# The MLP's second product of the chunk pairs by seven block products

## Chip, cores and metric

One core of one Trainium2 chip. The metric is the device time of one execution in microseconds; before the change the median of three runs is 830.9 us. Engines are named as in the profile: PE (TensorE), DVE (VectorE), ACT (ScalarE), POOL (GpSimd), SP (SyncE, which issues nearly all DMAs here).

## The reference

Attention with a window of 64 positions, then a mixer: two products over the tokens, then two over the channels. All data are float32.

```python
x = attention(q, k, v)                    # (8, 576, 512)
h = np.maximum(xt @ w_tok1, 0.0) @ w_tok2
u = x + h.transpose(0, 2, 1)
h2 = np.maximum(u @ w_ch1, 0.0) @ w_ch2   # 512 -> 1536 -> 512
return (u + h2)
```

## The kernel before the change

The attention and the token products take the first 257 us or so. What follows is the channel MLP: `u` is cut into nine chunks of 512 tokens, kept in DRAM as `u_dram[j]` with the 512 channels as four blocks of 128 partitions.

**Precision.** A float32 operand is split into a high part in the type that PE takes (`hi`, a copy on ACT that rounds) and a low part (`lo` = operand - `hi`, a subtraction on DVE). A block product is three matmuls: weight hi x data hi, weight hi x data lo, weight lo x data hi. Weights are 128x128, data 128x512, and a product of 128x512 fills one PSUM bank of eight.

**Plain chunks** (0, 1, 2): `gemm1` makes hidden block `ft` (of 12) from four channel blocks, 12 matmuls; `relu_split` makes the hi and lo parts of its ReLU on ACT and DVE. `gemm2` sums over hidden blocks into the four output blocks, and `add_out` adds them to `u` and stores. While chunk 1 runs, a generator (`weight_steps`) makes the sums of `w1` that the next part needs, a step after each hidden block, and stores them as `w1s` in DRAM.

**Chunk pairs** (3,4), (5,6), (7,8): here the first product is already done by Strassen's scheme in Winograd's form. The 2x2 blocks are channel halves, hidden halves and the two chunks; seven products `m1` to `m7` take the place of eight. `pair_f(q, f)` makes the four hidden blocks (`f` and `f + 6`, of each chunk) with 7 x 6 = 42 matmuls in four banks P, Q, R, S, in the order m1, m6, m7, m5, m2, m4, m3. Products share banks: `m2` is accumulated on top of `m1` in P, `m4` on `m7` in R, `m3` on `m5` in S. So the bank must have been read before the later product starts: x1 (a copy of P by ACT), x1 + Q, x2 = x1 + R, x3 = x2 + S, and later x2, x1 again, all on DVE. The data operands of the seven products (`comb`, tags c0 to c6) are hi and lo parts of sums of `u` blocks: `load_raw` loads raw blocks, `sums` and `sum4` form the sums on DVE, `prep` splits them. For the next pair this is done in the last f of a pair and in the second product behind it.

After every two f (a **group**, three in a pair) comes the second product as before Strassen: eight outputs (two chunks, four channel blocks) in eight banks, each a sum over the four hidden blocks made, 8 x 4 x 3 = 96 matmuls, and eight `add_out`. The whole of `w2` stays in SBUF as hi and lo parts (`w2hi`, `w2lo`).

**Order.** The program's order on each engine is that in which the code is written; nothing is moved. Each engine works strictly in its order, and a DMA waits in SP's order. `w1s` comes in slots of one f (three of them, `load_w1`, two DMAs of 896 KB), loaded again when its f is done.

## Time and profile before

| | |
|---|---|
| runs | 829.18, 830.9, 831.1 us |
| profiled execution | 829.17 us, its span 827.4 us, granted PE clock 0.999 |
| attention and token products | to about 257 us |
| chunk 0 | about 257 to 324 us |
| chunks 1, 2 | 324.2 to 389.5 and 389.5 to 454.7 us |
| pairs | 454.7, 577.8 and 700.8 us, the last to the end |
| HBM traffic | 164 GB/s over the span |

The profile gives the busy time of each engine, groups of equal instructions with mean duration and the idle time before them, a timeline, windows (busy time of each engine in a stretch), and the chain of waits that ended last. Matmuls overlap, so the duration of one (0.39 us) is longer than the distance from one to the next.

### The profile page before, as it was taken

To read this page: it belongs to the slowest core of one execution; us is meant where nothing else is said; L and a number is where in the kernel's file an instruction comes from. 1 tells how busy PE (TensorE), PEld (TensorE's weight loads), DVE (VectorE), ACT (ScalarE), POOL (GpSimd) and SP (SyncE) were. 2 spreads that over 40 slices of the span, in tenths; PEclk is the share of its full clock that TensorE was granted. 3 is DMA by queue.
4 is the path that set the end of the run, shared out by engine and by line. 5 is a ranking of instruction groups with operands and counts; after the bars stand their busy time and mean duration, and the time that the engine had idled before them with its cause. 6 is when DMAs were issued, how large, how long until landed. Compare 5 with 4: busy or idle time off the path is not lost.

```text
span 827.4 us, 15250 instructions
## 1 busy us (share of the span) xinstructions
PE 814.4 (98%) x5860; PEld 676.9 (82%) x5860; DVE 511.1 (62%) x1365; ACT 336.6 (41%) x1014; POOL 106.5 (13%) x117
## 2 busy tenths in 40 slices
PE   8989999999999999999999999999999999999998
PEld 6758888888889878888888888878888878888886
DVE  5987899799773993773444535277625277525352
ACT  6988989888864530331221202032202033202020
POOL 3632534444330000000000000000000000000000
PEclk9999999999999999999999999999999999999999
DMA  9847778777645629634506443334433234432002
GB/s 354 284 148 243 237 243 291 231 228 276 193 132 174 193 65 273 185 96 136 182 1 237 143 180 111 118 111 171 170 159 135 95 131 167 176 137 90 1 1 101
DMA packets 69672, 136.51 MB, mean 165 GB/s; under 512 B 7008, under 2 KB 39264, under 8 KB 67680
## 3 DMA queue, kind: packets, MB, share of 16 engines
q1 hardware_dynamic: 67488, 133.71, 47.4%
q10 hardware_dynamic: 2112, 1.84, 0.7%
q8 instruction: 46, 0.75, 0.4%
q14 instruction: 26, 0.21, 0.1%
HBM read 104.66 MB, written 30.87 MB: 164 GB/s over the span
## 4 chain that ended last, share of the span: by engine, by line
PE 84%; DVE 8%; ACT 4%; issue 2%; DMA 1%; POOL 0%; POOLq 0%; DVEq 0%; SPq 0%; ACTq 0%
PE gp L847 19%; PE op L635 11%; PE gp L627 8%; PE h L364 5%; PE up L412 5%; PE op_4a L635 4%; PE op_2b L635 4%; PE op_2a L635 4%; PE op_0b L635 4%; PE op_0a L635 4%; PE op_4b L635 4%; PE xp L316 4%; PE s L274 3%; PE pp L304 3%; PE up L405 2%; ACT e L297 2%
## 5 line engine op out<-in xcount | busy, mean ns | idle before, releaser
L847 PE MATMUL gp<-m,w1hi 128*128 128x512 f32 x504 | 155.3, 390 | 0.7 <-DVE x L855 0.7
L297 ACT ACTIVATE e<-e,nm 128x128 f32<-128x128 f32 x288 | 112.2, 397 | 6.5 <-DVE nm L289 6.3
L847 PEld LDWEIGHTS gp<-m,w1hi 128*128 128x128 f32 x504 | 94.5, 188 | 21.0 <-DVE x L855 1.5
L847 PE MATMUL gp<-m,w1lo 128*128 128x512 f32 x252 | 98.0, 389 | 0.0
L614 ACT ACTIVATE ghi<-x 128x512 fp32r<-128x512 f32 x54 | 34.1, 632 | 119.9 <-DVE x L857 68.3
L289 DVE CUSTOM_DVE_ANT_0 e<-s,mask 128x128 f32<-128x128 f32 x288 | 65.3, 285 | 10.6 <-PE s L274 10.5
L851 ACT COPY x<-gp 128x512 f32<-128x512 f32 x18 | 10.4, 578 | 143.3 <-PE gp L847 143.3
L615 DVE SCALAR_TENSOR_TENSOR glo<-x,ghi 128x512 fp32r<-128x512 f32 x54 | 37.4, 692 | 38.1 <-ACT ghi L614 38.1
L614 ACT ACTIVATE ghi<-gp 128x512 fp32r<-128x512 f32 x50 | 29.9, 597 | 70.0 <-PE gp L627 70.0
L627 PE MATMUL gp<-uhi,w1lo 128*128 128x512 f32 x144 | 56.0, 389 | 0.0
L627 PE MATMUL gp<-ulo,w1hi 128*128 128x512 f32 x144 | 56.0, 389 | 0.0
L627 PE MATMUL gp<-uhi,w1hi 128*128 128x512 f32 x144 | 56.0, 389 | 0.0
L297 ACT ACTIVATION_READ_ACCUMULATOR e<-e,nm 128x1 f32 x288 | 55.9, 194 | 0.0
L847 PEld LDWEIGHTS gp<-m,w1lo 128*128 128x128 f32 x252 | 47.3, 188 | 9.9
L615 DVE SCALAR_TENSOR_TENSOR glo<-gp,ghi 128x512 fp32r<-128x512 f32 x50 | 34.4, 688 | 25.4 <-ACT ghi L614 25.3
L635 PE MATMUL op<-glo,w2hi 128*128 128x512 f32 x128 | 49.8, 389 | 0.0
L635 PE MATMUL op<-ghi,w2hi 128*128 128x512 f32 x128 | 49.8, 389 | 0.0
L635 PE MATMUL op<-ghi,w2lo 128*128 128x512 f32 x128 | 49.8, 389 | 0.0
L316 PEld LDWEIGHTS xp<-v,pt 128*64 128x64 f32 x1152 | 36.6, 138 | 12.9 <-ACT e L297 9.4
L104 POOL TENSOR_TENSOR xlo<-x,xhi 128x512 fp32r<-128x512 f32 x32 | 41.6, 1300 | 43.6 <-ACT xhi L101 42.9
L304 PE MATMUL pp<-ident,e 128*128 128x128 f32 x288 | 45.4, 282 | 1.5
L274 PE MATMUL s<-k,q 64*64 64x128 f32 x1152 | 41.8, 277 | 2.6 <-DMA k<-kh 0.9
(161 smaller groups left out, 1827.9 us busy)
## 6 DMA issues: line engine op xcount, KB each, us to landing
v<-vh SPq DMA_DIRECT2D x36, 512.0 KB, 4.4
w1hi<-w1s SPq DMA_DIRECT2D x18, 896.0 KB, 4.7
w1lo<-w1s SPq DMA_DIRECT2D x18, 896.0 KB, 6.5
raw<-wc SPq DMA_DIRECT2D x32, 384.0 KB, 4.6
q<-qh SPq DMA_DIRECT2D x36, 256.0 KB, 4.7
k<-kh SPq DMA_DIRECT2D x7, 1280.0 KB, 7.7
out<-uf SPq DMA_DIRECT2D x35, 256.0 KB, 2.7
uf<-u_dram SPq DMA_DIRECT2D x8, 1024.0 KB, 9.1
```

What stands on the lines that cost most here:

```text
L104: eng_lo.tensor_sub(lo, src, hi.bitcast(F32))
L274: nc.tensor.matmul(so, qt[r, j, half], kbs[b][r, n:n + 2, j], start=True, stop=True)
L289: nc.vector.tensor_tensor_reduce(out=e[:, h], in0=s[:, h], in1=mk, scale=-scale, scalar=MAX_F32, op0=ALU.add, op1=ALU.min, accum_out=nm[:, ...
L297: nc.scalar.activation(e[:, h], e[:, h], AF.Exp, bias=nm[:, g:g + 1], scale=-1.0, accum_out=sm[:, g:g + 1])
L304: nc.tensor.transpose(pp[:, h], e[:, h], ident)
L316: nc.tensor.matmul(xp[half * BLK:(half + 1) * BLK, h], pts[h % 2][:, h // 2, half * BLK:(half + 1) * BLK], vt[:, half, h], start=True, sto ...
L364: nc.tensor.matmul(h_ps[b][tt], w[:, o + tt * P:o + (tt + 1) * P], x, start=first and n == 0, stop=last and n == len(combos) - 1)
L614: nc.scalar.activation(hi, src, AF.Relu)
L615: nc.vector.scalar_tensor_tensor(out=lo, in0=src, scalar=0.0, in1=hi.bitcast(F32), op0=ALU.max, op1=ALU.subtract)
L627: nc.tensor.matmul(gp, w[:, w1_at(ft, ct)], x[:, ct], start=(k == 0), stop=(k == 3 * NCT - 1))
L635: nc.tensor.matmul(op, w[:, ct, ft], x[:, cols], start=(first and k == 0), stop=(last and k == 3 * len(gs) - 1), skip_group_check=not (fir ...
L847: nc.tensor.matmul(b, w[:, at], c[:, h, t], start=(n < 4 and k == 0), stop=(k == 5), skip_group_check=True)
```

## The change

The second product of the pairs is done by the same seven products: blocks are output channel halves (t counts the two blocks in a half), hidden halves and chunks. A group takes 2 (t) x 7 x 2 (f) x 3 = 84 matmuls (`pair_op`), t = 0 in banks of the even set, t = 1 of the odd one, with the same sharing of banks. The seven data operands are sums of the four hidden blocks of an f:

- `block` takes the ReLU of a hidden block into SBUF as float32 (`made`: r11, r12, r22, r21; the names that the rows show as `w2hi_r` and `w2lo_r`, in room that the end of `w2` leaves). For m1, m2, m3 it also makes the hi part (ACT) and the lo part (DVE for m1, POOL for m2 and m3).
- `combine(fi)` makes the other four (sums t1, t2, r12 - in place - and t1 again on DVE, their hi parts on ACT, their lo parts on DVE). For the even f it runs step by step between the products of the odd f, for the odd f at once in the second product, behind the products that need only the even f.
- Parts that two t's and groups share are added into `ufs` as banks are read; m1 + m6 is kept in `common` and added to three outputs only in the last group (by POOL, at the program's end by DVE). There are 14 reads of banks in a group, and 6 more additions in the last.

The sums of `w2` are made in chunk 1 (`weight_steps2`, 31 steps, from `w2_dram`, which now gets all of `w2`), its plain quarters are stored in chunk 2 (`quarter_steps2`), and `load_w2s` brings a slot for each t and group, two DMAs of 896 KB. `w1` has two slots instead of three. `Columns` is a tensor in several tiles, so that a part can be used again by itself. Half of the lo parts of `prep` for the next pair go to POOL.

```diff
-SLOT, NSLOT = NPROD * 2 * P, 3
+SLOT, NSLOT = NPROD * 2 * P, 2
+NGRP = NH // 2
...
+        def weight_steps2():
...
+                nc.vector.tensor_add(s1, s1, a)
+                hi("m5")
+                yield
+                nc.vector.tensor_sub(a, c, a)
+                hi("m7")
+                lo("m5")
+                yield
...
+        def load_w2s(n):
+            if n < (NCHUNK - N_PLAIN) // 2 * NGRP * 2:
+                grp, t = n // 2 % NGRP, n % 2
+                for k, w in enumerate((w2hf, w2lf)):
+                    nc.sync.dma_start(w[:, t * SLOT:(t + 1) * SLOT].bitcast(F32),
+                                      w2s[k][:, grp, t].rearrange("p m f c -> p (m f c)"))
...
                     if j == 1:
                         next(steps, None)
+                        if half == 1 and ft % 2:
+                            next(steps2, None)
+                    if last and half == 0:
+                        next(steps3, None)
...
-                    load_w1(2)
...
                     if j == 1:
                         next(steps, None)
+                        for _ in range((2, 5)[half]):
+                            next(steps2, None)
...
+        def combine(fi):
+            r, sub = made, nc.vector.tensor_sub
+            sub(r["t1"], r["r12"], r["r11"])
+            parts_hi(fi, "m5")
+            yield
+            sub(r["t2"], r["r22"], r["t1"])
+            parts_hi(fi, "m6")
+            yield
+            sub(r["r12"], r["r22"], r["r12"])
+            parts_hi(fi, "m7")
+            yield
+            parts_lo(fi, "m6", nc.vector)
+            yield
+            parts_lo(fi, "m5", nc.vector)
+            yield
+            sub(r["t1"], r["r21"], r["t2"])
+            parts_hi(fi, "m4")
+            yield
+            parts_lo(fi, "m7", nc.vector)
+            yield
+            parts_lo(fi, "m4", nc.vector)
...
+            def block(name, src, m, eng):
+                nc.scalar.activation(made[name], src, AF.Relu)
+                if m:
+                    parts_hi(fi, m)
+                    parts_lo(fi, m, eng)
...
                     nc.vector.tensor_add(x3, b, x2)
-                    done(1, f + NH, x3)
+                    block("r22", x3, "m3", nc.gpsimd)
                 elif m == "m2":
-                    done(0, f, b)
+                    block("r11", b, "m1", nc.vector)
                 elif m == "m4":
                     nc.vector.tensor_add(x2, b, x1)
-                    done(0, f + NH, x2)
+                    block("r21", x2, "m2", nc.gpsimd)
                 else:
                     nc.vector.tensor_add(x1, b, x1)
-                    done(1, f, x1)
+                    block("r12", x1, None, None)
+                next(rest, None)
+                if q + 1 < len(pairs):
+                    if f == NH - 2 and m == "m1":
+                        sums()
+                    if f == NH - 1 and n < 4:
+                        prep(q + 1, m, 0, nc.gpsimd if n % 2 else nc.vector)
+        def pair_op(q, grp, ufs, more, final):
...
+            for t in range(2):
+                for fi in range(2):
+                    product(t, "m1", fi)
+            for m in PRODUCTS[1:4]:
+                for t in range(2):
+                    product(t, m, 0)
+            for _ in combine(1):
+                pass
+            if more:
+                for m in PRODUCTS[4:]:
+                    if m == "m4":
+                        sum4()
+                    prep(q + 1, m, 0, nc.gpsimd if m == "m4" else nc.vector)
+                load_raw(q + 1, 1)
+            for t in range(2):
...
+                    if m != "m1" and (m != "m2" or not end):
+                        for fi in (1,) if m in PRODUCTS[:4] else (0, 1):
+                            product(t, m, fi)
+                    if m == "m1" and grp == 0:
+                        nc.scalar.copy(common[t], b)
+                    elif m in ("m1", "m6"):
+                        nc.vector.tensor_add(common[t], b, common[t])
+                    elif m == "m7":
+                        add(1, 2 + t, b)
...
+                    if more and t == 1 and m == "m1":
+                        sums()
+                    if more and t == 1:
+                        if m == "m4":
+                            sum4()
+                        prep(q + 1, m, 1, nc.gpsimd if m in ("m7", "m2", "m3") else nc.vector)
+                load_w2s((q * NGRP + grp + 1) * 2 + t)
```

How the order moves, at three places. First DVE in the odd f of the first pair's second group (f = 3), before:

```order
L853 TENSOR_TENSOR x_0_3_6418<-gp_3_1_6415,x_0_3_6418 128x512
L855 TENSOR_TENSOR x_0_3_6419<-gp_3_2_6416,x_0_3_6418 128x512
L857 TENSOR_TENSOR x_0_3_6420<-gp_3_3_6417,x_0_3_6419 128x512
L615 SCALAR_TENSOR_TENSOR glo_9_6450<-x_0_3_6420,ghi_9_6449 128x512
L615 SCALAR_TENSOR_TENSOR glo_3_6460<-gp_3_0_6414,ghi_3_6459 128x512
L862 TENSOR_TENSOR x_0_3_6419<-gp_3_2_6416,x_0_3_6418 128x512
L615 SCALAR_TENSOR_TENSOR glo_9_6471<-x_0_3_6419,ghi_9_6470 128x512
L865 TENSOR_TENSOR x_0_3_6418<-gp_3_3_6417,x_0_3_6418 128x512
```

Now the same stretch begins with the even f's `combine` (L964 to L977 are its sums, L959 a lo part, `gp` a bank of the f):

```order
L964 TENSOR_TENSOR w2lo_r<-w2hi_r 128x512
L967 TENSOR_TENSOR w2lo_r<-w2hi_r,w2lo_r 128x512
L1011 TENSOR_TENSOR x_1_6268<-gp_3_1_6612,x_1_6268 128x512
L970 TENSOR_TENSOR w2hi_r<-w2hi_r 128x512
L1013 TENSOR_TENSOR x_0_6269<-gp_3_2_6613,x_1_6268 128x512
L959 TENSOR_TENSOR gloc_6254<-w2lo_r,ghic_6253 128x512
L1015 TENSOR_TENSOR x_0_6270<-gp_3_3_6614,x_0_6269 128x512
L959 TENSOR_TENSOR gloc_6258<-w2lo_r,ghic_6257 128x512
L959 TENSOR_TENSOR w1lo_69<-w2hi_r,w1hi_67 128x512
L977 TENSOR_TENSOR w2lo_r<-w2hi_r,w2lo_r 128x512
L1020 TENSOR_TENSOR x_0_6269<-gp_3_2_6613,x_1_6268 128x512
L959 TENSOR_TENSOR gloc_6256<-w2hi_r,ghic_6255 128x512
```

Between the five reads of banks stand nine other instructions now (two more rows, L1023 and L959, end the f), where there were four lo parts.

Second ACT in the last f of the first pair (f = 5), before (`m` is a hi part for the next pair, `ghi` one of a hidden block):

```order
L851 COPY x_0_5_6686<-gp_5_0_6682 128x512
L101 CAST m_1_6699<-r_1_0_6599 128x512
L101 CAST m_1_6709<-t_1_0_6608 128x512
L101 CAST m_1_6719<-r_1_0_6601 128x512
L614 ACTIVATE ghi_11_6729<-x_0_5_6688 128x512
L101 CAST m_1_6733<-t_1_0_6607 128x512
L614 ACTIVATE ghi_5_6742<-gp_5_0_6682 128x512
```

and now (L955 is a hi part for the second product, L126 one for the next pair, L991 a ReLU into `made`):

```order
L991 ACTIVATE w2hi_r<-x_0_6267 128x512
L955 CAST ghic_6257<-w2lo_r 128x512
L1009 COPY x_1_6268<-gp_5_0_6876 128x512
L955 CAST ghic_6253<-w2lo_r 128x512
L126 CAST m_1_6891<-r_1_0_6537 128x512
L955 CAST ghic_6255<-w2hi_r 128x512
L126 CAST m_1_6903<-t_1_0_6546 128x512
L126 CAST m_1_6914<-r_1_0_6539 128x512
L991 ACTIVATE w2hi_r<-x_0_6270 128x512
L955 CAST w2hi_4552<-w2hi_r 128x512
L126 CAST m_1_6928<-t_1_0_6545 128x512
L991 ACTIVATE w2hi_r<-gp_5_0_6876 128x512
```

The copy of bank P and the ReLUs stand behind hi parts that wait for DVE's sums.

Third DVE in the second product of that last group, before: the eight reads of banks stood alone behind the preps. Now, from the end of `combine(1)` on (L129 a lo part for the next pair, L857 `sum4`, L1077 and L1045 reads of banks of t = 0):

```order
L959 TENSOR_TENSOR gloc_6266<-w2lo_r,ghic_6265 128x512
L129 TENSOR_TENSOR m_1_7014<-r_1_0_6543,m_1_7014 128x512
L857 TENSOR_TENSOR r_1_0_6537<-r_1_0_6543,t_1_0_6546 128x512
L129 TENSOR_TENSOR m_1_7021<-r_1_0_6541,m_1_7021 128x512
L1077 TENSOR_TENSOR w2lo_r<-op_2_0_0_6964,w2lo_r 128x512
L1077 TENSOR_TENSOR w2lo_r<-op_2_0_1_6965,w2lo_r 128x512
L1045 TENSOR_TENSOR uf_6335<-op_2_0_2_6966,uf_6335 128x512
L1045 TENSOR_TENSOR uf_6335<-op_2_0_3_6967,uf_6335 128x512
```

PE's products m2, m4 and m3 of t = 0 go into the banks that the fifth, seventh and eighth row read, and wait for them.

More of the change, by code (lines that the diff above doesn't have):

```diff
@@ L633, in gemm2 @@
             for ft, (ghi, glo) in zip(fts, gs):
-                for w, x in ((w2hi, ghi), (w2hi, glo), (w2lo, ghi)):
-                    nc.tensor.matmul(op, w[:, ct, ft], x[:, cols], start=(first and k == 0),
+                at = slice((ct * NFT + ft) * P, (ct * NFT + ft + 1) * P)
+                for w, x in ((w2hf, ghi), (w2hf, glo), (w2lf, ghi)):
+                    nc.tensor.matmul(op, w[:, at], x[:, cols], start=(first and k == 0),
                                      stop=(last and k == 3 * len(gs) - 1), skip_group_check=not (first and last))
@@ new lines, in mixer_kernel @@
+        whole = [t[:, n] for t in whole for n in range(4)]
+        behind = [[w[:, NSLOT * SLOT + n * CHUNK:NSLOT * SLOT + (n + 1) * CHUNK] for n in range(5)] for w in (w1hi, w1lo)]
+        behind += [w[:, NSLOT * SLOT:NSLOT * SLOT + CHUNK] for w in (w2hf, w2lf)]
+        spare = [new_g(f"c{n}") for n in range(8)]
+        ops_g = [dict(zip(PRODUCTS, spare[:7])),
+                 dict(zip(PRODUCTS, [*zip(behind[0], behind[1]), spare[7], tuple(behind[2:])]))]
+        made = dict(zip(("r11", "r12", "r22", "r21", "t1", "t2"), whole))
```

194 lines of the change are left out of this document (139 added, 55 removed).

## Prediction

> **What bounds the kernel now.** I read the page first, then the chain that ended last, then the engines' rows in the pairs.
>
> ```profile
> PE 814.4 (98%) x5860; PEld 676.9 (82%) x5860; DVE 511.1 (62%) x1365; ACT 336.6 (41%) x1014; POOL 106.5 (13%) x117
> ...
> 700.80 19.04 PE gp L847 x84
> 719.84 5.44 PE op_0a L635 x24
> ...
> 736.16 5.44 PE op_0b L635 x24
> 741.60 19.04 PE gp L847 x84
> ```
>
> The first row is the page's, the others are the chain of waits of the third pair's first group. TensorE is the bound and never waits there: two f take 19.04 us for 84 matmuls, the second product 4 x 5.44 = 21.76 us for 96. That is **0.2267 us a matmul**. The mean of 390 ns that the page gives counts overlapping matmuls, and a saving worked out with it would be too large by 1.7.
>
> ```profile
> 454.70:577.80 123.10, 122.76 (x542) 101.35 (x541) 64.44 (x99) 25.82 (x44) 0.00 (x0) 1.00 0.38 137
> 577.80:700.80 123.00, 122.66 (x541) 101.27 (x540) 65.62 (x101) 25.82 (x44) 0.00 (x0) 1.00 0.40 142
> 700.80:822.00 121.20, 121.20 (x538) 100.39 (x537) 53.26 (x80) 18.17 (x30) 0.00 (x0) 1.00 0.23 86
> ```
>
> These are windows of the three pairs (length, then PE, PEld, DVE, ACT, POOL busy). DVE has half its time free and POOL all of it; only in the first two pairs does PE lose 0.34 us.
>
> **What goes.** The second product of a group falls from 96 matmuls to 84, over nine groups 108 matmuls: 108 x 0.2267 = **24.5 us less**. The profiled execution took 829.2 us (span 827.4 and 1.8 around it; the median shown is 830.9), so without new waits 804.7.
>
> **What comes in the pairs.** The order rows show it. A group's DVE had 18 + 8 = 26 instructions; now 2 x 14 + 14 = 42, of which 18 have two SBUF inputs. Their pace:
>
> ```profile
> 548.53 0.68 DVE L745 TENSOR_TENSOR t<-r,r 128x512 f32<-128x512 f32 x1
> 549.25 0.69 DVE L747 TENSOR_TENSOR r<-r,r 128x512 f32<-128x512 f32 x1
> 549.85 0.69 DVE L748 TENSOR_TENSOR t<-r,t 128x512 f32<-128x512 f32 x1
> ...
> 551.66 0.68 DVE L104 TENSOR_TENSOR m<-t,m 128x512 fp32r<-128x512 f32 x1
> 552.26 0.69 DVE L855 TENSOR_TENSOR x<-gp,x 128x512 f32<-128x512 f32 x1
> ```
> ```profile
> 553.00 0.74 PE L847 MATMUL gp<-m,w1hi 128*128 128x512 f32 x2 [0.34 <-DVE x L855]
> ```
>
> DVE starts one every 0.60 us, 0.72 where it needs the one before; PE starts 0.05 us after the DVE instruction that it waits for (552.26 + 0.69 to 553.00). So 42 x 0.60 = 25 us fit in the group's new 38.1 us (168 x 0.2267). **As a sum the work fits; as a chain it does not.** The chain runs over ScalarE:
>
> ```profile
> 553.46 0.69 DVE L857 TENSOR_TENSOR x<-gp,x 128x512 f32<-128x512 f32 x1
> 554.84 0.69 DVE L615 SCALAR_TENSOR_TENSOR glo<-x,ghi 128x512 fp32r<-128x512 f32 x1 [0.70 <-ACT ghi L614]
> ```
> ```profile
> 554.18 0.63 ACT L614 ACTIVATE ghi<-x 128x512 fp32r<-128x512 f32 x1 [2.41 <-DVE x L857]
> 554.72 0.60 ACT L101 CAST m<-t 128x512 fp32r<-128x512 f32 x1
> 555.23 0.59 ACT L614 ACTIVATE ghi<-gp 128x512 fp32r<-128x512 f32 x1
> ```
>
> ACT starts one every 0.52 us, lasts 0.6, and a hand-over between ACT and DVE costs 0.03. From the end of a product to DVE it is 0.25 us.
>
> *Ordinary group* (seven of nine), time 0 at the first matmul of its odd f. Bank R must be read before m4 at 6.8, S before m3 at 8.2; the second product starts at 9.5, the products that need the odd f's sums at 16.3, and it should end at 28.6. DVE's order: the even f's last sum ends at 1.25, ACT's ReLU of it at 2.5 (behind another ReLU and a copy), `t1` at 3.2; then six instructions, one of them waiting for ACT's copy of m1, until x3 at 7.5. ACT then has ReLU, copy, ReLU, copy before DVE's low part of m1 can start: it ends at 10.7, with DVE idle from 8.1. Four more: x1 at 13.1, its ReLU at 13.7. Then `combine(1)`, eight in a row, `t1` at 14.5, the low part of m7 at 18.5, of m4 at 19.2, and only then the reads of the second product's banks: m1 at 19.8, m7 at 21.2. PE would need m7's low part at 17.2 and the read of m1 at 18.4: it is 1.5 us late at the end of the group.
>
> **POOL's new work.** The low parts of m2 and m3 go to POOL, four a group. What that does to DVE is seen in the attention stage:
>
> ```profile
> 125.49 1.05 DVE L327 SCALAR_TENSOR_TENSOR ri<-sum 128x8 f32<-128x8 f32 x1
> ```
> ```profile
> 123.96 1.00 POOL L213 TENSOR_TENSOR w<-r,c 128x384 f32<-128x384 f32 x1 [1.55 <-DVE r L211]
> 125.25 1.28 POOL L104 TENSOR_TENSOR xlo<-x,xhi 128x512 fp32r<-128x512 f32 x1 [0.28 <-ACT xhi L101]
> ```
> ```profile
> L327 DVE SCALAR_TENSOR_TENSOR ri<-sum x29: 161/918/1291, 52.5 to 238.6; 128x8 f32<-128x8 f32 x29
> ```
> ```profile
> 123.80 0.68 DVE L333 TENSOR_TENSOR x<-xp,ri 128x512 f32<-128x512 f32 x1
> ```
> ```profile
> L104 DVE TENSOR_TENSOR t2lo<-w,t2hi x3: 559/1506/1516, 40.0 to 59.5; 128x384 fp32r<-128x384 f32 x3
> ```
>
> An eight-column instruction with both inputs in SBUF takes 0.16 us at best and 0.92 in the median, and ends when POOL's does (126.54 and 126.53). The low part of t2 takes 0.56 or 1.51. L333, with an input in PSUM, is not held (0.68 beside 1.00 of POOL). So a low part or a sum that meets one of POOL's 1.28 us is held until POOL ends, then needs some 0.55. In the chain above this happens three times: POOL works from 2.0 to 3.3 (`t1` ends at 3.85), from 9.5 to 10.8 (low part of m1 at 11.3) and from 14.3 to 15.6 (`t1` at 16.15). Then m7's low part ends at 20.2 and the read of m1 at 21.5, and the group at 31.8: **3.2 us late**. Bounds of an ordinary group: 0 and 5.3 (1.5 and three times 1.28). I take 3.2, since three kinds of rows show DVE held.
>
> The Trainium skill, *SBUF — State Buffer*, section *Who interferes with whom*, says that a VectorE instruction with two SBUF inputs and a GpSimd instruction that reads SBUF exclude each other for the whole instruction, and that the later one waits. The trace agrees for VectorE (1.05 us above). By its worst case, 1.28 us for each meeting, the sum would be 872; the sum here does not use it.
>
> *Transition* (the last group of the first two pairs). Its DVE has 16 in the odd f and 33 in the second product; POOL has 12 more. With no meeting, the next pair's m1 part waits for ACT until 6.1, so x2 ends at 8.0 (m4 1.2 late) and x3 at 10.4 (m3 2.3 late); m1's low part ends at 14.2, `combine(1)` and three preps at 25.8, the read of m1 at 26.4 where PE has waited since 23.1; behind t=0 come three sums, two preps and the read of m6 before m7 is read at 36.5, PE waiting since 33.9. The group ends at 39.6: 11 us late. With POOL's meetings the same marks are 8.6, 11.7, 16.1, 29.5, 30.1 and 40.8, and the end is 43.6: **15 us late**. The nearest row is the 0.34 us above, where the same preps stood beside five sums and four low parts, and none of the sums waited for a ReLU. Bounds: DVE at 0.60 without a gap, 41 instructions from 2.5 to 27.1 for a read due at 25.8, is 1.3 late; four more whole instructions of POOL make 20. Below nothing neither term can go: PE waits for nothing in the pairs that the change could take away but the 0.34.
>
> **What is hidden.**
>
> ```profile
> w1hi<-w1s SPq DMA_DIRECT2D x18, 896.0 KB, 4.7
> w1lo<-w1s SPq DMA_DIRECT2D x18, 896.0 KB, 6.5
> ...
> r<-u_dram SPq DMA_DIRECT2D x28, 256.0 KB, 3.8
> ...
> w1s<-wlo_m SPq DMA_DIRECT2D x16, 192.0 KB, 2.2
> ```
> ```profile
> 324.20:389.50 65.30, 65.30 (x289) 54.06 (x289) 40.29 (x73) 16.77 (x32) 0.00 (x0) 1.00 0.50 149
> ```
>
> The 36 new loads of `w2s` are of this size and have 19 to 28 us from the end of one use to the next; two slots of `w1` instead of three still leave 28. Cost 0; if a load came late, its lateness. The reload of the raw blocks starts on SP once the transition's last prep has read them (29.5) and takes 3.8: 33.5, and DVE comes to them at 36.5. In the second chunk 48 instructions of 128x256 come to DVE. One of that size stands at the program's end:
>
> ```profile
> 824.08 0.42 DVE L640 TENSOR_TENSOR uf<-op_4b,uf 128x256 f32<-128x256 f32 x1 [1.07 <-PE op_4b L635]
> ```
>
> That is 20 us on 40.3 of 65.3. Of 31 steps 20 lie in the last 16.3 us, and 48 stores, 2.2 us each to landing, stand on SP between them: I put the end some 4 us late, 8 at most, and the next chunk has four banks of 2.72 us each. I take 0 (bounds 0 and 2). The 14 stores of quarters in the third chunk stand on SP around its raw loads, 4.7 MB in 16 us; those blocks are wanted only some 9 us later: 0. The 11 more stores of converted `w2` in the first chunk wait for what DVE has just made: 0. The end of the program keeps its two halves: 0.
>
> **Sum.** 829.2 - 24.5 + 7 x 3.2 + 2 x 15 = **857 us**.
>
> **Rivals.**
> - *POOL and DVE do not meet* (POOL falls into DVE's idle stretches, of which the chain has several): 829.2 - 24.5 + 7 x 1.5 + 2 x 11 = 837. Against it: in two of the three places POOL and DVE are released by the same ACT instructions.
> - *The saving stands.* DVE and ACT keep their pace and the waits fall on stretches with room: only the dense bound is left, 829.2 - 24.5 + 2 x 1.3 = 807. For it: before, 20 DVE instructions in such an f cost 0.34. Against it: now each sum waits for a ReLU on ACT before the next may start. It holds if the read of m1 in the second product ends before 18.4 in both kinds of group.
> - *The weights' sums block the second chunk*: if they end over 9 us late there, PE waits for banks: some 5 us more, 862.
>
> **How the numbers follow.** The forecast has 0.46, no meeting 0.20, the saving 0.22, the second chunk 0.05, and 0.07 lies near no change. The range leaves out the saving: from 822 (no meeting, ordinary groups free, transitions 8.5 us late) to 868 (one whole POOL instruction more in each ordinary group, 9 us, and 2 of the second chunk). A measurement tells 0.3% (2.5 us) from no change: faster 0.24, same 0.07, slower 0.69.
>
> **What would show it.** Right: PE busy in the pairs falls by about 24 us, yet each of the first two pairs is longer than 123 us by 9 or more; PE waits before the second product's matmuls for DVE's reads of banks and low parts; DVE instructions with two SBUF inputs last over 1 us beside POOL's. Wrong, and then how: no DVE instruction over 0.8 us in the pairs (the first rival); pairs of 114 to 118 us (the second); idle time of PE between 324 and 455 (the third). A wait of PE for `w2s` or of DVE for raw blocks would mean that a load I hid is not hidden.

## The result and the profile after

The changed kernel takes **888.6 us** (median of four, 886.7 to 892.6) beside 830.0 for the kernel before: ratio **1.071**, 95% interval 1.067 to 1.076. The forecast was 857. The direction was right, the size was not: 32 us more were lost than forecast. The profiled execution is the slowest of the four, 892.6 us with a span of 890.6.

The page of after, engines and the clock row of the 40 slices:

```profile
PE 830.0 (93%) x5752; PEld 666.2 (75%) x5752; DVE 630.7 (71%) x1545; ACT 422.7 (47%) x1173; POOL 191.1 (21%) x181
...
PEclk9999999999999999989899999997999989999999
```

TensorE has the 108 matmuls less (5752 for 5860), yet more busy time than before (814.4), and its clock has dips. Both are one thing, as windows of after show (length, PE, PEld, DVE, ACT, POOL busy, granted clock, DMA share, GB/s): the three plain chunks, the three pairs, and two short stretches.

```profile
260.20:331.00 70.80, 67.78 (x291) 55.13 (x290) 47.67 (x102) 21.48 (x45) 0.00 (x0) 0.98 0.61 187
331.00:404.50 73.50, 69.19 (x289) 55.63 (x288) 50.81 (x104) 23.15 (x48) 0.00 (x0) 0.95 0.71 211
404.50:477.20 72.70, 69.17 (x289) 55.28 (x289) 34.77 (x61) 17.32 (x34) 0.00 (x0) 0.95 0.70 242
477.20:619.10 141.90, 125.48 (x505) 96.86 (x504) 98.31 (x140) 51.20 (x88) 29.72 (x22) 0.95 0.56 204
619.10:759.40 140.30, 125.84 (x506) 97.08 (x505) 99.51 (x140) 50.43 (x88) 31.41 (x25) 0.95 0.56 201
759.40:887.40 128.00, 120.64 (x511) 93.53 (x509) 89.34 (x130) 44.76 (x76) 23.34 (x18) 1.00 0.45 166
```
```profile
388.00:392.00 4.00, 3.38 (x7) 2.44 (x8) 3.31 (x8) 1.18 (x4) 0.00 (x0) 0.50 0.74 206
392.00:396.00 4.00, 4.00 (x14) 3.15 (x13) 2.99 (x8) 1.52 (x4) 0.00 (x0) 0.70 0.85 234
396.00:400.00 4.00, 4.00 (x19) 3.31 (x18) 1.22 (x3) 0.16 (x1) 0.00 (x0) 1.00 0.96 317
```

The plain chunks took 66.6, 65.3 and 65.3 us before; now each is late, by 4, 8 and 7. Around 390 TensorE runs at half its clock: 7 matmuls in 3.38 us, where at clock 1.00 there are 19 in 4. The timeline of after shows what goes before such a stretch (start, duration, instruction, in brackets the wait):

```profile
596.23 0.40 PE L1041 MATMUL op<-w1hi,w2lo 128*128 128x512 f32 x1
600.35 0.80 PE L1041 MATMUL op<-ghic,w2hi 128*128 128x512 f32 x1 [3.73 <-DVE w2lo_r L1077]
600.95 0.63 PE L1041 MATMUL op<-gloc,w2hi 128*128 128x512 f32 x1
601.37 0.63 PE L1041 MATMUL op<-ghic,w2lo 128*128 128x512 f32 x1
...
606.07 0.40 PE L1041 MATMUL op<-gloc,w2hi 128*128 128x512 f32 x1
606.30 0.40 PE L1041 MATMUL op<-ghic,w2lo 128*128 128x512 f32 x1
```

A wait of 3.73 us, then thirteen matmuls about 0.43 us apart, then again 0.23. Busy time times (1 - granted clock), added up in windows of one us, gives an estimate of 19.5 us lost in this way from 250 us on: 7.5 before the pairs, 12.0 in the two transitions, none in the ordinary groups. Before the change there was none.

Where the 63.2 us between the two spans (827.4 and 890.6) lie, by the first matmuls of the stages:

| | forecast | measured | of it halved clock |
|---|---|---|---|
| 108 matmuls less | -24.5 | -24.5 | |
| attention, start of chunk 0 (257.4 before, 260.2) | 0 | 2.8 | |
| three plain chunks (197.1 before, 217.0) | 0 | 19.9 | 7.5 |
| seven ordinary groups (six of 41.7 us for 38.1, the last 5.4 late) | 22.4 | 27.1 | |
| two transitions (58.7 and 56.7 for 38.7) | 30 | 38.0 | 12.0 |

The start of chunk 0 moved between 256.5 and 260.2 over the experiments, whatever they changed, so the 2.8 are not counted as the change's.

### The profile page after: what moved, and what is told of

It reads as the page before. It is cut to its first block, busy times and chain, and to the rows that moved or that the text cites. A ratio compares the mean times of both kernels' runs of the same rounds, so it can differ in the third digit from the quotient of the medians.

```text
span 890.6 us, 15820 instructions
## 1 busy us (share of the span) xinstructions
PE 830.0 (93%) x5752; PEld 666.2 (75%) x5752; DVE 630.7 (71%) x1545; ACT 422.7 (47%) x1173; POOL 191.1 (21%) x181
## 4 chain that ended last, share of the span: by engine, by line
PE 21%; DVE 16%; ACT 13%; issue 4%; DMA 4%; SPq 1%; ACTq 0%; DVEq 0%
PE op L1041 11%; PE gp L1005 5%; ACT w2hi_r L991 5%; ACT ghic L955 4%; DVE w2lo_r L964 3%; DVE w1lo L959 3%; PE op L665 3%; ACT w1hi L955 2%; PE gp L656 2%; DMA out<-uf 2%; DVE x L1015 1%; DVE w2lo_r L977 1%; DVE m L129 1%; DMA w2t<-w_dram 1%; DVE w2lo_r L967 1%
## 5 line engine op out<-in xcount | busy, mean ns | idle before, releaser
L1005 PE MATMUL gp<-m,w1hi 128*128 128x512 f32 x504 | 158.3, 396 | 7.8 <-DVE x L1013 5.3
L959 POOL TENSOR_TENSOR gloc<-w2hi_r,ghic 128x512 fp32r<-128x512 f32 x18 | 23.2, 1292 | 411.7 <-ACT ghic L955 404.3
L1045 DVE TENSOR_TENSOR uf<-op,uf 128x512 f32<-128x512 f32 (+1 forms) x91 | 61.6, 683 | 28.4 <-PE op L1041 26.3
L1041 PE MATMUL op<-ghic,w2hi 128*128 128x512 f32 (+1 forms) x145 | 60.2, 415 | 15.4 <-DVE uf L1045 7.9
L321 DVE CUSTOM_DVE_ANT_0 e<-s,mask 128x128 f32<-128x128 f32 x288 | 65.3, 285 | 12.1 <-PE s L306 12.0
L991 ACT ACTIVATE w2hi_r<-x 128x512 f32<-128x512 f32 x54 | 34.1, 631 | 65.2 <-DVE x L1015 47.1
L1041 PE MATMUL op<-gloc,w2hi 128*128 128x512 f32 (+1 forms) x145 | 58.7, 405 | 0.0
L1041 PE MATMUL op<-ghic,w2lo 128*128 128x512 f32 (+1 forms) x145 | 58.7, 405 | 0.0
L665 PE MATMUL op<-ghi,w2hi 128*128 128x512 f32 x128 | 53.0, 414 | 5.3 <-ACT ghi L643 5.3
L656 PE MATMUL gp<-uhi,w1hi 128*128 128x512 f32 x144 | 56.1, 390 | 0.1
L665 PE MATMUL op<-glo,w2hi 128*128 128x512 f32 x128 | 53.1, 414 | 2.5 <-DVE glo L644 2.5
L1041 PE MATMUL op<-w1lo,w2hi 128*128 128x512 f32 (+1 forms) x91 | 38.8, 426 | 14.0 <-DVE w1lo L959 14.0
L129 POOL TENSOR_TENSOR xlo<-x,xhi 128x512 fp32r<-128x512 f32 x32 | 41.6, 1300 | 45.3 <-ACT xhi L126 44.6
```

Of the source, the lines that this page charges most:

```text
L129: eng_lo.tensor_sub(lo, src, hi.bitcast(F32))
L321: nc.vector.tensor_tensor_reduce(out=e[:, h], in0=s[:, h], in1=mk, scale=-scale, scalar=MAX_F32, op0=ALU.add, op1=ALU.min, accum_out=nm[:, ...
L656: nc.tensor.matmul(gp, w[:, w1_at(ft, ct)], x[:, ct], start=(k == 0), stop=(k == 3 * NCT - 1))
L665: nc.tensor.matmul(op, w[:, at], x[:, cols], start=(first and k == 0), stop=(last and k == 3 * len(gs) - 1), skip_group_check=not (first a ...
L959: eng.tensor_sub(lo, made[MADE[m]], hi.bitcast(F32))
L991: nc.scalar.activation(made[name], src, AF.Relu)
```

## The experiments

All are measured beside the kernel before. *Plain* is the time from the first matmul of chunk 0 to that of the pairs, *group* the usual period of an ordinary group, *transitions* the first and the second, all from the profiled execution. Each ratio is to the runs of the kernel before that stood beside it (medians of 828.6 to 830.0 us). From f7_all on the group behind a transition is longer than the usual one, about 40 us or more.

| run | us | ratio (95%) | plain | group | transitions |
|---|---|---|---|---|---|
| before | 830.0 | 1 | 197.1 | 40.8 | 41.4, 41.4 |
| after | 888.6 | 1.071 (1.067 to 1.076) | 217.0 | 41.7 | 58.7, 56.7 |
| e1_no_sums_no_stores | 869.6 | 1.050 (1.048 to 1.051) | 197.4 | 41.7 | 56.0, 58.7 |
| e2_no_sums | 871.1 | 1.052 (1.050 to 1.054) | 200.9 | 41.7 | 55.3, 58.7 |
| f6_w3 | 886.8 | 1.070 (1.067 to 1.073) | 213.2 | 41.7 | 58.9, 56.6 |
| x1_two_loads | 881.1 | 1.062 (1.059 to 1.066) | 209.3 | 41.7 | 56.5, 56.7 |
| x2_no_w2s_stores | 882.8 | 1.063 (1.061 to 1.065) | 209.1 | 41.7 | 56.6, 56.6 |
| f1_spread | 887.4 | 1.071 (1.068 to 1.073) | 217.0 | 41.7 | 56.1, 56.2 |
| f5_banks | 887.2 | 1.070 (1.068 to 1.072) | 213.6 | 41.7 | 56.1, 58.8 |
| e3_pool_lo_out | 871.7 | 1.052 (1.050 to 1.053) | 217.0 | 39.8 | 54.0, 56.4 |
| f3_lo_dve | 902.6 | 1.089 (1.085 to 1.092) | 216.6 | 43.2 | 57.0, 57.1 |
| e4_zero_matmuls | 881.1 | 1.064 (1.062 to 1.065) | 216.2 | 41.7 | 53.7, 53.8 |
| f2_order | 851.6 | 1.027 (1.026 to 1.029) | 217.7 | 38.1 | 51.6, 50.9 |
| f7_all | 839.4 | 1.013 (1.012 to 1.015) | 210.1 | 38.1 | 46.5, 46.6 |
| f8_split | 829.5 | 1.000 (0.999 to 1.001) | 200.0 | 38.1 | 46.3, 46.6 |
| f9_reads | 832.0 | 1.003 (1.001 to 1.004) | 200.1 | 38.1 | 41.0, 41.4 |
| f10_lag | **825.9** | **0.996 (0.995 to 0.998)** | 200.0 | 38.1 | 45.0, 45.1 |
| f11_fill | 835.0 | 1.007 (1.006 to 1.008) | 199.8 | 38.1 | 44.9, 45.0 |
| f12_lag_fill | 829.5 | 1.001 (0.999 to 1.002) | 201.1 | 38.1 | 43.4, 43.4 |

### The weights' sums in the plain chunks

**e1_no_sums_no_stores.** Edit:

```diff
-steps, steps2, steps3 = weight_steps(), weight_steps2(), quarter_steps2()
+steps, steps2, steps3 = weight_steps(), iter(()), iter(())
-                                      w2s[k][:, grp, t].rearrange("p m f c -> p (m f c)"))
+                                      w1s[k][:, 2 * grp + t].rearrange("p m t c -> p (m t c)"))
-                    if src is wc2:
-                        nc.sync.dma_start(w2_dram[:, o:o + m], w)
```

> After the change, without anything that makes the second product's combined weights in the plain chunks: no sums in the second chunk, no quarter stores in the third, no 11 extra stores of converted w2 in the first. The pairs load the first product's combined weights in their place (same size, same time of issue), so the output is not the reference's. Theory A (the plain chunks lose their 20 us to that work alone): the three chunks take 66.6, 65.3 and 65.3 us again, the pairs begin at about 457 instead of 477, the clock stays at 1.00 there, and the time is 888.6 - 20 = 868 to 869. Rival B (the lateness comes from what stays: tiles cut in columns, two slots, POOL): the pairs begin at 470 or later, 880 to 889.

869.6 us: theory A, 0.6 above its range. The chunks take 66.9, 65.3 and 65.3 us, the clock stays at 1.00 in them, the pairs begin at 455.0.

**e2_no_sums.** As above, but the third edit and `quarter_steps2` are left as in the changed kernel.

> As the run without sums and stores, but the 11 stores of converted w2 and the quarter stores of the third chunk stay. Theory A1 (the stores are free, the sums with their loads cost it all): 868 to 869, as without the stores. Rival A2 (the stores block VectorE's tiles in the first chunk, 4.2 us, and hold the queue in the third): 873 to 880, with the first chunk at 70.7 us and the third above 68.

871.1 us lies between the two: A2 is right for the first chunk, which stays at 70.3 us, A1 for the second and third, which take 65.3. So the sums with their loads and stores cost 217.0 - 200.9 = 16 us, the stores of the third chunk nothing, the 11 stores of converted weights 3.5. How, the waits of e2's VectorE show (engine, instruction, what it waited for: us in total, times, longest):

```profile
DVE w L243 <- DMA w_dram<-w: 3.6, 4, 1.5
```

**f6_w3.** The conversion writes into two buffers in turn, and each is now held until its store has landed.

```diff
-w = cpool[0].tile([P, CW], F32, name=f"w{tag}", tag="cvw", bufs=2)
+w = cpool[0].tile([P, CW], F32, name=f"w{tag}", tag="cvw", bufs=3)
```

> After the change, with three buffers instead of two for the converted weights of the first chunk. Theory A (VectorE waits for the 11 added stores to give the buffer back, which makes one low part late, then the clock falls): first chunk 66.6 to 67.5 us instead of 70.7, 884.5 to 885.5. Rival B (the stores delay something else): 70 us and more, 888.

The first chunk takes 66.6 us, at clock 1.00: theory A. The median, 886.8, cannot be told from 888.6; its runs reach from 883.3 to 888.9.

**x1_two_loads, x2_no_w2s_stores.**

In `load` (x1) and in `store` (x2) of `weight_steps2`:

```diff
-                if n < 2 * NGRP:
+                if n < 2:
```
```diff
-                    for k in range(2):
+                    for k in range(0):
```

Both load `w1s` in place of `w2s`, as e1 does.

> After the change, with the sums of the weights made as often as before, but only the first two of their twelve loads of 512 KB issued; the pairs load the first product's weights in place of the sums, so the output is not the reference's. Theory A (VectorE waits in its queue for these loads, and what stands behind it is late): pairs begin at 459 to 464, 871 to 876. Rival B (the engines' own hand-overs, copy after sum after copy, cost it): pairs begin at 470 or later, 882 to 888.

> After the change, with the sums of the weights and all their loads, but none of the 96 stores of their parts; the pairs load the first product's weights in their place, so the output is not the reference's. Theory A (the stores hold SyncE's queue, so that the next load starts late, and hold the one buffer of the parts): pairs begin at 459 to 464, 871 to 876. Rival B (the hand-overs between VectorE and ScalarE cost it): pairs begin at 470 or later, 882 to 888.

x1 took 881.1 us, between its theories; x2 took 882.8, the time of its rival, with the pairs from 468.4 on. There are six loads and 48 stores (`w2t<-w_dram` x6, `w2s<-w2p` x48 among the DMA issues of after), not the twelve and 96 of the two expectations. The first chunk, which neither edit touches, took between 68.7 and 71.8 us in the runs with two buffers and the added stores, so the second and third are compared alone: 146.3 us together in after, 130.6 in e2, 140.3 in x1, 138.8 in x2. By that the loads cost 6.0 us and the stores 7.5 of 15.7. Each edit frees the third chunk (67.0 and 65.3 us) and leaves the second at 73 to 74. What stays with neither of them was not tried. The waits of after from 331 to 430 name both sides of it:

```profile
DVE w2t L786 <- DMA w2t<-w_dram: 12.4, 4, 5.6
ACT w2p L775 <- DVE uf L670: 11.5, 3, 4.5
ACT w2p L775 <- DVE w2t L786: 9.9, 3, 6.7
```

and the chain of waits of after, at the end of the second chunk and into the third, how it comes to TensorE:

```profile
394.68 4.71 DMA out<-uf
...
399.83 4.82 DMA w2t<-w_dram
404.67 0.42 DVE w2t L786
...
405.82 4.85 DMA w2t<-w_dram
410.73 3.14 DMA w2s<-w2p
413.97 0.41 ACT w2p L775
414.38 0.51 ACT ghi L643
414.91 1.29 DVE glo L644 x2
```

A load (`w2t`) stands in SyncE's queue behind eight stores of the parts, for which SyncE needs 4.4 us (395.36 to 399.78, 0.55 us each). VectorE waits in its queue for the load (5.6 us at the longest), ScalarE's copy (`w2p`) waits for VectorE or for the store that still reads its buffer. Behind that copy stands the ReLU of the third chunk's hidden block (`ghi`), due long ago. The sums themselves are cheap; they stand in the same queues as what TensorE needs.

**f1_spread, f5_banks.** The same steps at other places of the second chunk; in both `weight_steps2` yields once behind its first two loads. f1:

```diff
-                        if half == 1 and ft % 2:
-                            next(steps2, None)
+                        next(steps2, None)
...
-                        for _ in range((2, 5)[half]):
+                        for _ in range((3, 2)[half]):
                             next(steps2, None)
```

f5, which also has a second buffer for the parts:

```diff
-                        if half == 1 and ft % 2:
+                        if ft == 0 or half == 1 and ft < NH + 4:
                             next(steps2, None)
...
-                        for _ in range((2, 5)[half]):
+                        for _ in range((4, 3)[half]):
                             next(steps2, None)
```

> After the change, with the same sums of the weights spread over the whole second chunk: the first loads are issued at its first f, then one step at each f and three or two at each bank of the second product, instead of 20 of 31 steps in its last 16 us. Theory A (it is their crowding at the chunk's end, behind loads and stores, that costs the plain chunks 15 us): second and third chunk at 65.3 to 66.5 us, pairs begin at 459 to 462, 871 to 874. Rival B (the work costs the same wherever it stands): pairs begin at 470 or later, 882 to 889.

> After the change, with the same sums of the weights beside the second chunk's second products in the main: loads issued at the chunk's first f, four steps at each bank of the first half, one at each of the next four f, three at each bank of the second half, and two buffers for what is stored. Theory A (the sums cost through the queues: a ReLU or its low part stands behind a copy that waits, so it matters that none is due there): second and third chunk together 131 to 136 us instead of 146, pairs begin at 459 to 466, 871 to 879. Rival B (each of the 30 steps costs its share wherever it stands): pairs begin at 472 or later, 884 to 889.

By their times both are rival B. Crowding alone was not the cause, though f5's second and third chunk took 140.0 us together, between the 131 to 136 of its theory A and the 146.3 of after. Spread evenly, the third chunk is clean and the second pays all of it (windows of f1_spread):

```profile
330.00:410.60 80.60, 70.77 (x290) 55.04 (x290) 57.05 (x120) 26.11 (x56) 0.00 (x0) 0.94 0.77 234
410.60:475.90 65.30, 65.30 (x290) 54.07 (x289) 28.94 (x45) 14.50 (x26) 0.00 (x0) 1.00 0.62 214
```

VectorE has 57 us of work for a chunk of 65.3 (before it had 40.3, the sums of the first product's weights among them). With so little left, waits in its queue make ReLUs late; that is argued from the rows, and f8 below bears it out.

### The order and POOL in the pairs

**e3_pool_lo_out, f3_lo_dve.** What POOL's low parts cost, and what the same parts cost on VectorE:

```diff
-                    parts_lo(fi, m, eng)
+                    if eng is nc.vector or (q == 0 and f < 2):
+                        parts_lo(fi, m, eng)
```
```diff
-                    parts_lo(fi, m, eng)
+                    parts_lo(fi, m, nc.vector)
```

> After the change, with POOL's low parts of m2 and m3 made only in the first group of the first pair; the later groups use those old ones, so the output is not the reference's. VectorE and ScalarE do what they did. Theory A (POOL holds VectorE in each ordinary group by some 2.2 us): periods of ordinary groups fall from 41.8 to about 39.6 us, transitions by 2 to 4 us each, 888.6 - 7 x 2.2 - 6 = 867. Rival B (the chain over ScalarE alone makes the lateness): periods stay at 41.8, 886 to 889.

> After the change, with only this other: the low parts of m2 and m3 stand on VectorE in the place where POOL had them, right behind ScalarE's copy. POOL then holds nobody in ordinary groups, VectorE has 46 instructions instead of 42 and waits for ScalarE twice more in each f. Theory A (a wait in VectorE's queue costs as much as POOL's hold): each ordinary period 42.3 to 45 us, 891 to 915. Rival B (the hold is the price, VectorE has the room): periods near 39.9 as in the run without these parts, 872 to 876.

Both as theory A. Without POOL's part a period is 39.8 us, 1.9 less; with the same parts on VectorE, each behind a wait for ScalarE, it is 43.2, 1.5 more than with POOL. The first sum of `combine` (L964) shows the hold, in the timeline of after, and then in the groups of instructions in the pairs (count, busy us, mean ns) of after, of e3 and of f2:

```profile
672.73 1.29 POOL L959 TENSOR_TENSOR gloc<-w2hi_r,ghic 128x512 fp32r<-128x512 f32 x1 [2.67 <-ACT ghic L955]
673.15 1.42 DVE L964 TENSOR_TENSOR w2lo_r<-w2hi_r 128x512 f32<-128x512 f32 x1 [1.15 <-ACT w2hi_r L991]
```
```profile
L964 DVE TENSOR_TENSOR w2lo_r<-w2hi_r 128x512 f32<-128x512 f32 x18 | 26.6, 1477 | 11.6 <-ACT w2hi_r L991 10.3
```
```profile
L964 DVE TENSOR_TENSOR w2lo_r<-w2hi_r 128x512 f32<-128x512 f32 x18 | 14.0, 777 | 10.8 <-ACT w2hi_r L991 9.8
```
```profile
L964 DVE TENSOR_TENSOR w2lo_r<-w2hi_r 128x512 f32<-128x512 f32 x18 | 12.4, 687 | 0.1
```

POOL ends at 674.02, VectorE at 674.57, 0.55 later, as the prediction had it. Of 18 such sums the mean is 1.48 us in after and 0.69 in f2, where POOL is idle in these groups. That agrees with the rule of the Trainium skill, *SBUF — State Buffer*, section *Who interferes with whom*, that the prediction weighed. m1's low part, the third meeting that the prediction counts in an ordinary group, took 0.78 us instead of 0.68 there and was hardly held.

**f2_order.** Nothing is taken away: the order is another, and POOL's low parts of m2 and m3 go to VectorE, as in f3. In the transitions the next pair's second sums and parts move along with the reads of banks. `due` is what the product before put into `pend`, and `both(m, fi)` makes the product for both t. What follows the rows below is then made and read in the order m2, m6, m7, m5, m4, m3, each for both t:

```diff
                 if m:
                     parts_hi(fi, m)
-                    parts_lo(fi, m, eng)
+                    pend.append(m)
...
                 next(rest, None)
+                for x in due:
+                    parts_lo(fi, x, nc.vector)
...
-            for t in range(2):
-                for fi in range(2):
-                    product(t, "m1", fi)
-            for m in PRODUCTS[1:4]:
-                for t in range(2):
-                    product(t, m, 0)
-            for _ in combine(1):
-                pass
+            both("m1", 0)
+            both("m6", 0)
+            both("m1", 1)
+            both("m7", 0)
+            both("m5", 0)
+            rest = combine(1)
+            for _ in range(4):
+                next(rest)
+            for t in range(2):
+                if grp == 0:
+                    nc.scalar.copy(common[t], bank[t][0])
+                else:
+                    nc.vector.tensor_add(common[t], bank[t][0], common[t])
+            for _ in rest:
+                pass
```

> After the change, with the pair groups put in another order and all low parts of m1, m2 and m3 on VectorE, each one product later than its ScalarE copy; the second product runs m1, m6, m7, m5 of the even f, then m2, and only then what needs the odd f's sums; bank reads of m1 stand in the middle of those sums. As many instructions as before, POOL free in ordinary groups. Theory A (the lateness is the order: VectorE waits in its queue for ScalarE, is held by POOL, and reads banks too late): ordinary periods fall from 41.8 to 38.3 to 39.2 us, transitions from 57.7 to 50 to 53, 845 to 856. Rival B (VectorE and ScalarE are too slow for 42 and 24 instructions in any order): periods stay above 40.5, 872 or more.

Theory A. The chain of waits of f2 in the second pair is TensorE alone, and a window shows the engines in the first pair's second group:

```profile
640.95 19.04 PE gp L1008 x84
659.99 19.04 PE op L1046 x84
```
```profile
513.00:551.10 38.10, 38.10 (x169) 31.53 (x168) 29.82 (x46) 14.24 (x24) 0.00 (x0) 1.00 0.58 220
```

Ordinary groups take 38.08 us, exactly 168 matmuls of 0.2267, with VectorE at 29.8 us of 38.1 and POOL idle. So the 22 to 27 us that these groups lost came of order and not of too much work: the move to VectorE alone, in f3, made a group 1.5 us longer, and with the other order it is TensorE's 38.1. About half of the loss was POOL's hold (1.9 of 3.6 us, by e3), the rest VectorE's waits in its queue for ScalarE and late bank reads, which f2 does not tell apart.

### The halved clock

**e4_zero_matmuls.** In the last group of the first two pairs:

```diff
+            def fill(t, m, n):
+                for _ in range(n):
+                    nc.tensor.matmul(bank[t][INTO[m]], zmat, ops_g[0]["m1"][0], start=False, stop=False,
+                                     skip_group_check=True)
...
                         for fi in (1,) if m in PRODUCTS[:4] else (0, 1):
+                            if more and (t, m, fi) in ((0, "m5", 1), (1, "m2", 1)):
+                                fill(t, m, (16, 13)[t])
                             product(t, m, fi)
```

> After the change, with 58 matmuls more: in each of the two transitions 16 with zero weights ahead of the product that waits 3.7 us, and 13 ahead of the one that waits 3.0 us; they add zero to a bank. Theory A (TensorE's clock is halved after each of these two waits, and each halving costs 1.6 to 3 us of the path): no clock below 1.00 behind the filled waits, transitions shorter by 4 to 6 us each, 888.6 - 9 = 879 to 880. Rival B (the halved stretch behind the first wait is hidden by VectorE, which is late at the second wait in any case): only the second wait's halving is won, 883 to 885. Rival C (the clock falls for another reason, and 58 matmuls cost their 0.227 us where the wait was shorter): 888 to 895.

881.1 us lies between A and B; the trace decides for A. 58 matmuls more make the kernel 6 to 7.5 us faster (by the ratios 0.0076 of 829, by the medians 7.5). The second products of the two transitions take 29.5 and 29.6 us instead of 35.8 and 32.5: 6.3 and 2.9 less, where the halved stretches behind the two waits had cost 5.8 and 3.4. Windows of e4 in the first transition: two of its second product, where after had the thirteen slow matmuls, and one ahead of it:

```profile
580.00:586.00 6.00, 6.00 (x20) 4.36 (x19) 4.62 (x7) 3.57 (x7) 2.73 (x3) 0.74 0.72 254
...
595.00:600.00 5.00, 4.89 (x22) 3.63 (x21) 4.44 (x7) 0.62 (x1) 1.58 (x2) 1.00 0.63 197
600.00:605.00 5.00, 5.00 (x24) 4.14 (x23) 4.30 (x6) 0.00 (x0) 2.83 (x3) 1.00 0.76 242
```

The first row is what is missing to 879: behind a wait of 1.88 us in the odd f the clock fell here in both transitions, and the two f took 24.2 us instead of 23.0. In after it did so behind the same wait (1.89) in the second transition, not in the first.

### Putting the remedies together

**f7_all** has f2's order, f5's places of the sums, f6's third buffer, and in the transitions makes the next pair's second sums and parts only behind the reads of m7 and m5. **f8_split** adds this:

```diff
-                        if ft == 0 or half == 1 and ft < NH + 4:
+                        if ft == 0:
                             next(steps2, None)
...
-                        for _ in range((4, 3)[half]):
+                        for _ in range((3, 2)[half]):
                             next(steps2, None)
...
                     if last and half == 0:
                         next(steps3, None)
+                        next(steps2, None)
...
+                    if last and half == 0:
+                        for _ in range((2, 1, 1, 1)[ct]):
+                            next(steps2, None)
```

The first pair's parts of m7, m5 and m2, which need the same buffers, move from f 2 to f 6 and later.

> The other order of the pair groups, the sums of the weights beside the second chunk's second products, three buffers for converted weights, and in the transitions the bank reads of m7 and m5 ahead of the next pair's second sums and parts. If the four causes add (order 37 us, sums 10 to 15, first chunk 3, earlier reads 2 x 3): 825 to 832, the same as the kernel before. If the clock's falls or VectorE's sum in the transitions stay: 833 to 842.

> The run with all four remedies, and of the six sets of the weights' sums two made in the third chunk's first half, behind each ReLU there; the parts of the first pair that need the same buffers are made four f later. Theory A (VectorE, 87% busy in the second chunk, has no room for them there, and the third chunk has): second chunk 66 to 70 us, third at most 67, 827 to 832. Rival B (the hand-overs cost in the third chunk what they cost in the second): pairs begin at 467 or later, 837 to 842.

f7 took 839.4, in the second of its ranges: the second chunk still lost 12.9 us (78.2), 4.3 of them halved clock, and each transition nearly 8. f8 took 829.5, theory A: second chunk 68.1, third 65.3. A third of the steps moved out, and the second chunk's loss fell by 10 us.

**f9_reads, f10_lag, f11_fill, f12_lag_fill** go for the transitions. f10 makes the low parts of the next pair's m1 and m7 in the odd f one product after their copies (as `pend` above); f9 has that, reads banks R and S (m7, m5) first, P and Q after the next sums, and the low parts of m1 and m4 later; f11 is f8 with twelve zero matmuls before the product that waits 3.0 us there; f12 is f10 with them.

> The run split over two chunks, and in the two transitions VectorE reads the banks of m7 and m5 first, those of m2 and m6 after the next pair's second sums, and makes each low part of the next pair one step later than its copy. Theory A (what is left of the transitions' 8.2 us is the order of VectorE's queue: 1.6, 0.9, 3.2 and 1.6 us of waits and 1.5 of halved clock each): transitions of 39.5 to 42 instead of 46.3 us and no halved clock, 817 to 822. Rival B (VectorE's sum of instructions is the bound there, the waits only move): 826 to 830.

> The run split over two chunks, and of the reads run only this: in the last odd f of the first two pairs the low parts of the next pair's m1 and m7 one product later than their copies. Theory A (that wait of 1.6 us was the queue's order): second product of the transitions starts 2.1 us earlier and ends 1 to 2 us earlier, 825 to 828. Rival B (VectorE's sum is the bound, it gives the time back behind): 828.5 to 830.

> The run split over two chunks, with 12 matmuls of zero weights ahead of the product that waits 3.2 us in each transition. Theory A (the halved clock behind it costs 1.5 us of the path in each): clock 1.00 there, 826 to 827. Rival B (VectorE is late there at any clock): 829 to 830.

> Both edits together. Theory A for both: 823 to 826. Rival B for both: 829 to 830.

f9 is rival B by its mechanism, though 832.0 us is above its range: its transitions are 41.0 and 41.4 us, and the groups behind them 47.3 and 47.4 instead of 40.8 and 40.1 in f8. The waits moved over the border. f10 won 3 us (theory A) and is faster than the kernel before by 0.4%, 0.2 to 0.5. f11 missed both theories: the product itself ends 1.3 us earlier, but the next pair's first two f take 26.0 instead of 20.8 us, behind a wait of 2.95 us for VectorE, with the clock halved there (windows of f11):

```profile
585.00:588.00 3.00, 0.07 (x1) 0.00 (x0) 2.31 (x4) 1.62 (x3) 1.81 (x2) 0.85 0.34 128
588.00:592.00 4.00, 3.98 (x9) 3.14 (x10) 2.54 (x4) 0.29 (x1) 3.75 (x3) 0.50 0.41 156
```

f12 took 829.5, rival B: its transitions are 43.4 us instead of the 45.0 of f10, the groups behind them 43.9 and 44.0 instead of 40.0 and 40.3, each with a wait of 2.95 us for VectorE and halved clock behind it.

Our reading is that zero matmuls help where the wait's end is followed by work that TensorE bounds, as in e4. In f8 VectorE is the bound (39.3 us busy in the transition of 46.3, where TensorE needs 38.1), and a faster TensorE waits later, for as long again.

## Why the prediction was wrong

- **The saving**: right, 108 matmuls of 0.2267 us; f2's groups show it whole. The sign named for it, PE's busy time in the pairs falling by 24 us, did not come: it was 372.0 us for 366.6. Of the 30 us between, 12.0 are halved clock; the rest was not taken apart.
- **Ordinary groups, 3.2 us each**: right, 3.6 measured for six of them (the last 5.4, with the program's end). POOL's share, 1.7 forecast, was 1.9; that this fits is in part luck, since two of the three meetings cost about what was forecast and the third next to nothing.
- **No meeting / the saving stands** (rivals): refuted by the rows of L964 and by the periods. That the saving could stand with another order, f2 showed.
- **Transitions, 15 us each**: the mechanism was right, the size too small by 4 each. They were 19 late on average, of which 6 are halved clock; by that estimate 13 would remain without it.
- **The weights' sums in the second chunk, "I take 0 (bounds 0 and 2)"**: this is the step that failed. It set 20 us of VectorE's work against 25 us of free time, the very sum that the prediction rejects for the pairs. They cost 16 us (e2). The third rival named the mechanism, TensorE idle between 324 and 455, but gave it 5 us and a chance of 0.05, with only a late end in view. The waits inside, for loads and buffers, were not priced. "The 11 more stores wait for what DVE has just made: 0" failed too: it looked at what the stores wait for, not at who waits for their buffer (3.5 us).
- **The halved clock**: no term for it, 19.5 us in the trace. The forecast held waits of TensorE of several us in each transition and did not ask what they do to its pace. The rule is in the Trainium skill, *TensorE: Matmul & The Clock Gate*, Part 1: an idle window of about 3.4 us brings the array to half its clock until it has been busy for a window. It also says that the window runs freely. The trace agrees on the windows and not on the idle time. From 250 us to the last matmul every halved stretch of after lasts 3.41 or 6.83 us, and the starts of the first four (305.69, 387.61, 425.15, 599.24) lie 24, 11 and 51 periods of 3.413 us apart. But single waits of 1.89 to 3.74 us were enough. With the time cut into these periods in the 18 profiled runs from after on, every period at full clock in which TensorE was idle for 2.0 us or more is followed by a halved one, and none with less than 1.4 us is; between them both happen, as with the 1.89 us in the odd f. The trace of before could not show it, since TensorE hardly waited there.

The profiled execution, 892.6 us, missed the forecast by 35.6: 19.9 in the plain chunks, 8.0 in the transitions, 4.7 in the ordinary groups and the end, 2.8 before chunk 0. The median lies 4 us lower.

## What to carry to other kernels

Work that is to be hidden on a busy engine must be put into that engine's queue, not into its idle time: price each wait of its own (load, buffer, partner engine) by what stands behind it. Let a partner's result ripen for one step before the instruction that needs it, read banks before making what is needed later, and keep an order in which the product that depends on the latest sums comes last; together that was worth 37 us here (f2). And where TensorE will wait some 2 us or more at once, add a term for the clock.

## What the runs showed of the hardware

- Of the 85 halved stretches in these 18 runs, 38 lasted 3.41 us, 42 twice and 5 three times as long. By busy time times 0.5 the first cost 1.4 to 1.7 us, the second 2.0 to 3.2. The cost did not grow with the wait: 2.95 behind 3.0 us of waiting in after, 2.75 behind one of 7.2 us in f2. Single waits of 1.5 us (f8, odd f) did not halve the clock; one of 1.41 us in the second chunk did in f12 and not in f8 to f11.
- POOL's instructions with both inputs in SBUF took 1.29 or 1.43 us in ordinary groups of after and up to 1.74 in the transitions; VectorE's that met them took up to 1.65 instead of 0.69. Reads of banks were not held: 1.27 us for two beside POOL in f10 (581.5 to 582.8, POOL busy from 579.8 to 588.7).
